# Streaming weights from DRAM copies whose sixteenths lie 144 KB apart instead of 32 KB

## The chip, the cores and the metric

The kernel runs on one core of one Trainium2 chip. The metric is the device time of one execution in microseconds (us). A core has a matrix engine (PE; its weight loads are listed as PEld), a vector engine (DVE), a scalar engine (ACT), GpSimd (POOL) and a sync engine (SP). DMAs are issued by SP, ACT and POOL and carried out by the core's 16 DMA engines.

## The reference, cut to what matters

Two networks read the same normalised input `xn` and their results are added to `x`. Network A is an attention with a recurrent memory: 64 segments of 32 rows are worked off one after the other, since the first 8 output rows of a segment are the memory of the next. Network B computes a small gated MLP for two of the 2048 rows, picked by a router.

```python
for s in range(n_seg):                                   # 64 segments
    h = concatenate([mem, xn[:, 32*s:32*(s+1), :]])      # 40 rows x 1024
    q, k, v = h @ Wq, h @ Wk, h @ Wv                     # each 1024 x (32 heads * 128)
    p = softmax(where(mask, q @ k.T * scale, -1e9))
    o = einsum((p @ v), Wo)                              # (32*128) x 1024
    mem = o[:, :8, :]
    outs.append(o[:, 8:, :])
return x + concatenate(outs) + B(xn)
```

All four weight matrices are needed in each segment, because segment s+1 cannot begin before segment s has given its memory rows. [...]

## The kernel before

The weights are cut into 64 granules of 128 partitions x 2048 bf16 (512 KB). Granules 0 to 47 are pieces of Wq, Wk and Wv (a 128-row piece of the contraction times half of the 4096 columns, in the order of `PHASES`), granules 48 to 63 are two heads of Wo each. 44 granules stay in SBUF from the first segment on (tiles `wres`). The other 20, named in `STREAMED`, come from DRAM again in each segment. One of these (6) is kept in PSUM as a whole and half of another (25) as well, so from segment 1 on 18 whole granules and one half granule (256 KB) are streamed: 19 DMAs a segment, 63 segments.

The streamed granules go through five SBUF slots (pool `wstream`, `N_SLOT`, tile `g`). `fetch` (line 346) takes the next entry of the list `flow` and issues one DMA on SP's queue. In segment 0 it reads from the weight matrix itself (line 353), later from a DRAM copy of the granule, `wsc` (line 355). The call comes from `after` (line 460), as soon as the program has written down the last matmul that reads the granule which holds the slot, so SP's next issue waits for that matmul: the order of the fetches is the order of use, at most five granules ahead.

The copies `wsc` are DRAM tiles, made once in segment 0 by `copy_block` (line 385), one DMA from DRAM to DRAM each on POOL's queue. Each is [128, 2048]: the row that goes to partition p is 4 KB long and lies 4 KB behind that of partition p-1, so a copy is one contiguous block of 512 KB, and the eight rows of one sixteenth of the partitions (32 KB) stand next to each other. In the weight matrices Wq, Wk and Wv the rows of a granule are 8 KB apart, so there the rows of one sixteenth begin 64 KB behind those of the one ahead.

In a segment PE goes through the granules in order: for each of the six phases eight granules with four matmuls of 128x512 each (line 802), then 16 granules of Wo with eight of 128x256 (line 575). In between stand the transposes, scores and sums of the attention, and the projections of the memory rows of the group of segments to come (lines 568 and 587). Besides the granules, each segment moves small things: the input rows (line 273, POOL), the output rows (line 872, POOL), and a spill of projected rows (`ql_d`: stored from line 617 on ACT's queue, read back by line 484 on POOL). After the last segment the MLP's weights are loaded (lines 406 and 409) and used.

Of the kernel before, what the change touches and what calls it, by code (L numbers as in the profile page):

```python
# [8 lines left out]
BF16 = mybir.dt.bfloat16  # L9
# [41 lines left out]
def kernel(  # L51
# [16 lines left out]
    nc = tc.nc  # L68
    P = 128
    Bsz, S, D = A_x.shape  # L70
# [19 lines left out]
    Wo2 = A_Wo.rearrange("h e d -> (h e) d")  # L90
# [11 lines left out]
    def granule_dram(g):  # L102
        if g < 48:
            p, kc = divmod(g, KC)
            mat, half = PHASES[p]
            return Wqkv[mat][kc * P:(kc + 1) * P, 2048 * half:2048 * (half + 1)]
        w = g - 48
        return Wo2[2 * w * P:(2 * w + 2) * P, :].rearrange("(hh e) d -> e hh d", hh=2)

    def granule_out(t, g):  # L110
        return t[:, :] if g < 48 else t.rearrange("p (hh d) -> p hh d", hh=2)
# [3 lines left out]
    dram = ctx.enter_context(tc.tile_pool(name="dram", bufs=1, space=DRAM))  # L115
# [13 lines left out]
    def columns(g, s):  # L129
        if s > 0 and g == KEPT_WHOLE:  # L130
            return None
        return slice(0, 1024 if s > 0 and g == KEPT_PART else 2048)

    wsc = {g: dram.tile([P, columns(g, 1).stop - columns(g, 1).start], BF16, name=f"wsc{g}")
           for g in streamed if g != KEPT_WHOLE}
    r_d = dram.tile([1, S], BF16, name="r_d")

# [59 lines left out]
    for s in range(4):  # L197
        nc.vector.tensor_copy(out=SELM[:, s, :, 0:XM],
                              in_=IDENT[:, 32 * s:32 * s + XM].unsqueeze(1).to_broadcast([P, 4, XM]))
        nc.vector.tensor_copy(out=SELL[:, s, :, :],  # L200
                              in_=IDENT.rearrange("p (s c) -> p s c", c=32)[:, :, XM:SEG])
# [144 lines left out]
    def fetch():  # L346
        if not flow:
            return
        s, g = flow.pop(0)
        t = wstream.tile([P, 2048], BF16, tag="g", name="g")  # L350
        c = columns(g, s)
        if s == 0:
            nc.sync.dma_start(out=granule_out(t, g), in_=granule_dram(g))
        elif c is not None:
            nc.sync.dma_start(out=t[:, c], in_=wsc[g][:, :])
        queued.append((g, t))

    def part(t, jq):
# [26 lines left out]
    def copy_block(g):  # L385
        c = columns(g, 1)
        if c is not None:
            src = granule_dram(g)
            nc.gpsimd.dma_start(out=granule_out(wsc[g], g), in_=src if g >= 48 else src[:, c])

    to_copy = list(streamed)
    flow += [(s, g) for s in range(NSEG) for g in streamed if s == 0 or g != KEPT_WHOLE]
# [38 lines left out]
    for g in range(48):  # L431
        if g in streamed:
            n_q += 1
            if n_q < N_SLOT:
                fetch()
            continue
        if n_q >= N_SLOT:
            break
        load_resident(g)
        if g % 2 == 1 and n_x < NT // 2:  # L440
            load_x(n_x)
            n_x += 1
# [17 lines left out]
    def after(s, g):  # L460

        if s == 0:
            if g in side:
                side[g]()
            if g % 2 == 1 and g >= 8 and to_copy:
                copy_block(to_copy.pop(0))
            if n_x_left and g % 2 == 1:
                load_x(n_x_left.pop(0))
            while todo_res and todo_res[0] <= g + 2 * 64 // n_str + 8 and (todo_res[0] < resident[-10] or g >= 2 * NT + 12):
                load_resident(todo_res.pop(0))  # L470
        if g in streamed and (s == 0 or g != KEPT_WHOLE):
            fetch()
        if s == NSEG - 1:
            if g in resident:
                free_homes.append(g)
            if not flow:
                fetch_moe()
# [143 lines left out]
    for s in range(NSEG):  # L621
# [172 lines left out]
        for p, (mat, half) in enumerate(PHASES):  # L794
# [3 lines left out]
            for kc in range(KC):  # L798
                g = 8 * p + kc
# [198 lines left out]
```

## Time and profile before

| | |
|---|---|
| time, median of 3 runs | 1875.73 us (1872.84 to 1882.51) |
| the profiled execution | 1878.39 us, span 1876.7 us |
| PE busy | 1572.0 us, 84% of the span |
| DVE, ACT, POOL busy | 885.9, 692.0, 452.5 us |
| moved by DMA | 712.29 MB, mean 380 GB/s |
| of it on SP's queue (q1) | 671.18 MB |
| fetches from `wsc` | 1134 of 512 KB and 63 of 256 KB |

The span is the time from the first to the last instruction; the profiled execution is 1.7 us longer than its span. The row of DMA gives the busy share of the 16 DMA engines in tenths in 40 slices of 46.9 us, the row of GB/s what they moved. A DMA is listed with the time that its issue takes on the engine that issues it, and with the time from issue to landing.

### The profile page before, as it was taken

The numbers are of one execution on the slowest core, as the hardware profiler recorded it, in microseconds if no ns is written. First come the engines' busy times: TensorE is split into PE (matmuls) and PEld (weight loads), VectorE is DVE, ScalarE is ACT, GpSimd is POOL, SyncE is SP. The second block draws the span as 40 slices with busy tenths as digits, with TensorE's granted clock in tenths as the row PEclk, the third lists the DMA queues.
The fourth block names the chain that finished last, engine by engine and source line by source line (L and its number), as shares of the span: only waits on it lengthen the run. The fifth ranks groups of instructions, "written<-read, shape, count | busy, mean of one in ns | idle before, by whom it ended". The sixth has DMA issues, their size and how long they took to land.

```text
span 1876.7 us, 80489 instructions
## 1 busy us (share of the span) xinstructions
PE 1572.0 (84%) x34976; PEld 850.8 (45%) x34976; DVE 885.9 (47%) x2929; ACT 692.0 (37%) x1948; POOL 452.5 (24%) x898
## 2 busy tenths in 40 slices
PE   3458898889888988899889988988888888888864
PEld 1124444444454444445454444444444444444433
DVE  6725544544455444544454454544554454445430
ACT  1113433443344343444343344434343344334320
POOL 3111322213131322213131322323132221312120
PEclk8669999999999999999999999999999999999995
DMA  9999999999999999999999999999999999999998
GB/s 370 405 353 385 373 379 381 384 372 375 397 382 398 367 389 390 385 383 380 382 376 390 366 397 379 387 392 373 371 383 382 372 382 380 370 381 368 368 404 329
DMA packets 232115, 712.29 MB, mean 380 GB/s; under 512 B 39296, under 2 KB 53168, under 8 KB 231760
## 3 DMA queue, kind: packets, MB, share of 16 engines
q1 hardware_dynamic: 194384, 671.18, 93.4%
q0 software_dynamic: 28736, 28.09, 4.7%
q10 hardware_dynamic: 8640, 7.87, 1.2%
q8 instruction: 274, 4.49, 0.9%
q14 instruction: 81, 0.66, 0.1%
HBM read 694.32 MB, written 22.29 MB: 382 GB/s over the span
## 4 chain that ended last, share of the span: by engine, by line
DMA 57%; PE 37%; DVE 3%; issue 1%; ACT 1%; SPq 1%; ACTq 0%; DVEq 0%
DMA g<-wsc 50%; PE PSm L802 20%; PE PSl L568 5%; PE WO L575 4%; PE BT L638 3%; DMA XP<-in_A_x_dram 2%; PE WL L587 2%; DMA MW<-in_B_w_gate_dram 1%; DVE XR L248 1%; DMA MW<-in_B_w_up_dram 1%; DMA g<-in_A_Wq_dram 1%; DMA wres<-in_A_Wo_dram 1%; DMA g<-in_A_Wo_dram 1%; DMA MW<-in_B_w_down_dram 1%; DMA g<-in_B_w_down_dram 1%
## 5 line engine op out<-in xcount | busy, mean ns | idle before, releaser
L802 PE MATMUL PSm<-wres,ST 128*32 128x512 bf16 x8448 | 704.9, 384 | 7.8 <-DMA wres<-in_A_Wv_dram 3.6
L802 PEld LDWEIGHTS <-ST 128*32 128x32 bf16 x12288 | 323.0, 96 | 417.9 <-issue 174.7
L802 PE MATMUL PSm<-g,ST 128*32 128x512 bf16 x3588 | 361.4, 387 | 100.9 <-DMA g<-wsc 77.8
L575 PEld LDWEIGHTS <-OT 128*32 128x32 bf16 x8192 | 220.5, 97 | 162.8 <-issue 137.7
L821 ACT CAST XB<-PSm 128x512 bf16<-128x512 f32 x256 | 150.6, 588 | 293.2 <-PE PSm L802 290.9
L575 PE MATMUL WO<-wres,OT 128*32 128x256 bf16 x5632 | 238.6, 278 | 16.0 <-DMA wres<-in_A_Wo_dram 8.0
L484 POOL DMA_DIRECT2D LX<-ql_d x63 | 33.6, 533 | 816.0 <-PE WO L575 366.1
L575 PE MATMUL WO<-g,OT 128*32 128x256 bf16 x2560 | 132.7, 281 | 80.1 <-DMA g<-wsc 70.2
L568 PE MATMUL PSl<-wres,STL 128*32 128x512 bf16 x2112 | 184.0, 389 | 0.3 <-issue 0.2
L872 POOL DMA_DIRECT2D out_dram<-X x256 | 129.5, 513 | 215.0 <-DVE X L870 169.7
L653 DVE COPY KT<-BT 128x512 bf16<-128x512 bf16 x112 | 45.9, 410 | 286.5 <-issue 186.8
L273 POOL DMA_DIRECT2D X<-in_A_x_dram x256 | 129.5, 510 | 190.3 <-PE PSm L802 68.6
L378 ACT COPY BK<-KEPT 128x512 bf16<-128x512 bf16 x126 | 74.4, 590 | 130.0 <-PE WO L575 102.0
L646 ACT COPY QT<-BT 128x512 bf16<-128x512 bf16 x128 | 75.0, 586 | 125.9 <-PE BT L491 74.1
L638 PEld LDWEIGHTS <-XB 128*128 128x128 bf16 x1024 | 58.4, 98 | 117.8 <-ACT XB L821 67.9
L638 PE MATMUL BT<-IDENT,XB 128*128 128x128 bf16 x1024 | 102.0, 222 | 9.2 <-ACT XB L821 7.8
L568 PEld LDWEIGHTS <-STL 128*32 128x32 bf16 x3072 | 84.5, 98 | 55.7 <-issue 10.6
L870 DVE TENSOR_TENSOR X<-WO,X 128x256 bf16<-128x256 f32 x64 | 27.2, 425 | 170.4 <-PE WO L575 170.4
L831 ACT CAST VM<-PSm 128x512 bf16<-128x512 f32 x128 | 76.0, 594 | 85.0 <-PE PSm L802 83.8
L724 PEld LDWEIGHTS <-VM 32*128 32x128 bf16 x2048 | 65.5, 91 | 85.3 <-issue 72.2
L382 DVE COPY g<-KEPT 128x512 bf16<-128x512 bf16 x126 | 47.7, 420 | 108.5 <-PE PSm L802 62.0
L670 DVE TENSOR_TENSOR BS<-BS,CT 128x96 f32<-128x96 f32 (+1 forms) x256 | 59.1, 231 | 77.1 <-PE BS L663 72.7
(173 smaller groups left out, 2363.5 us busy)
## 6 DMA issues: line engine op xcount, KB each, us to landing
g<-wsc SPq DMA_DIRECT2D x1134, 512.0 KB, 6.1
g<-wsc SPq DMA_DIRECT2D x63, 256.0 KB, 5.5
LX<-ql_d POOLq DMA_DIRECT2D x63, 128.0 KB, 5.9
ql_d<-XBl ACTq DMA_DIRECT2D x60, 128.0 KB, 5.7
MW<-in_B_w_gate_dram SPq DMA_DIRECT2D x16, 448.0 KB, 9.5
MW<-in_B_w_up_dram SPq DMA_DIRECT2D x16, 448.0 KB, 9.0
wres<-in_A_Wk_dram SPq DMA_DIRECT2D x12, 512.0 KB, 11.6
MW<-in_B_w_down_dram SPq DMA_DIRECT2D x12, 512.0 KB, 10.6
```

What stands on the lines that cost most here:

```text
L273: nc.gpsimd.dma_start(out=X[s % 2][32 * g:32 * g + XM, :], in_=x2[s * SEG:s * SEG + XM, 256 * g:256 * (g + 1)])
L378: copy(out=back[c][:, :], in_=KEPT_COLS[KEPT_WHOLE][c])
L568: nc.tensor.matmul(PSl[32 * jq:32 * jq + 32, :], lhsT=STL[:, g % KC, :], rhs=part(Gv, jq), start=first_, stop=last_, tile_position=(0, 32 ...
L575: nc.tensor.matmul(PS[32 * g:32 * g + 32, 0:256], lhsT=lhs(h), rhs=Gv[:, D * hs + 256 * g:D * hs + 256 * (g + 1)], start=(first and hs == ...
L638: nc.tensor.transpose(out=PTq[:, il, :, :].rearrange("p j r -> p (j r)"), in_=XB[:, il * P:(il + 1) * P], identity=IDENT[:, :])
L646: nc.scalar.copy(out=QT[half][:, :, :], in_=pv)
L670: nc.vector.tensor_tensor(out=S4, in0=S4, in1=m, op=ALU.add)
L724: nc.tensor.matmul(o, lhsT=VM[half][q0:q0 + 32, il * P:(il + 1) * P], rhs=PTm[q0:q0 + 32, il, 0:NK], start=True, stop=False, tile_position ...
L802: nc.tensor.matmul(PSm[32 * jq:32 * jq + 32, :], lhsT=ST[:, kc, :], rhs=part(Gv, jq), start=(kc == 0), stop=(kc == KC - 1), tile_position= ...
L821: nc.scalar.copy(out=XB[:, :], in_=PSm[:, :])
L831: nc.scalar.copy(out=VM[half][:, :], in_=PSm[:, :])
L872: nc.gpsimd.dma_start(out=out2[s * SEG:s * SEG + XM, 256 * g:256 * (g + 1)], in_=OB[32 * g:32 * g + XM, :])
```

## The change

The DRAM copies get another shape. Each is now allocated as [16, 36, columns], of which rows 0 to 7 of each 36 are used. The eight rows of one sixteenth of the partitions stay contiguous (8 x 4 KB), and the next sixteenth begins 36 x 4 KB = 144 KB behind (72 KB for the half granule, whose rows are 2 KB; there it was 16 KB). The fetch reads the same 128 rows in the same order. The source of its DMA is now a pattern of three levels (16 x 8 x row) instead of two (128 x row). The copies of Wq, Wk and Wv granules stay one DMA each; those of the five Wo granules become two DMAs each, one for each of the two heads.

```diff
-    wsc = {g: dram.tile([P, columns(g, 1).stop - columns(g, 1).start], BF16, name=f"wsc{g}")
+
+    wsc = {g: dram.tile([16, 36, columns(g, 1).stop - columns(g, 1).start], BF16, name=f"wsc{g}")[:, 0:8, :]
            for g in streamed if g != KEPT_WHOLE}
...
         elif c is not None:
-            nc.sync.dma_start(out=t[:, c], in_=wsc[g][:, :])
+            nc.sync.dma_start(out=t[:, c], in_=wsc[g])
...
         if c is not None:
-            src = granule_dram(g)
-            nc.gpsimd.dma_start(out=granule_out(wsc[g], g), in_=src if g >= 48 else src[:, c])
+            if g >= 48:
+                w = g - 48
+                src = Wo2[2 * w * P:(2 * w + 2) * P, :].rearrange("(hh a b) d -> a b hh d", hh=2, b=8)
+                for hh in range(2):
+                    nc.gpsimd.dma_start(out=wsc[g][:, :, D * hh:D * (hh + 1)], in_=src[:, :, hh, :])
+            else:
+                nc.gpsimd.dma_start(out=wsc[g], in_=granule_dram(g)[:, c].rearrange("(a b) c -> a b c", b=8))
```

No instruction changes its place among the others of its engine. What changes is the form of the DMAs. On POOL, at the end of segment 0, the last copies stand so before the change (a row is the line, the destination, the source and the destination's pattern; `wsc_119` to `wsc_123` are the five Wo granules, `RROW` is the router's row):

```order
L389 DMA wsc_117<-in_A_Wv_dram 128x2048
L389 DMA wsc_118<-in_A_Wv_dram 128x2048
L389 DMA wsc_119<-in_A_Wo_dram 256x1x1024
L389 DMA wsc_120<-in_A_Wo_dram 256x1x1024
L260 DMA RROW<-r_d 1x16x128
L389 DMA wsc_121<-in_A_Wo_dram 256x1x1024
```

and so with it:

```order
L395 DMA wsc_117<-in_A_Wv_dram 16x8x2048
L395 DMA wsc_118<-in_A_Wv_dram 16x8x2048
L393 DMA wsc_119<-in_A_Wo_dram 16x8x1024 x2
L393 DMA wsc_120<-in_A_Wo_dram 16x8x1024 x2
L261 DMA RROW<-r_d 1x16x128
L393 DMA wsc_121<-in_A_Wo_dram 16x8x1024 x2
```

The five Wo copies are ten DMAs now, each with runs of 2 KB, 128 of them instead of 256. On SP, the first fetches of segment 1 stand so before the change (`wsc_105` to `wsc_109` are the first five streamed granules):

```order
L353 DMA g<-in_A_Wo_dram 128x2x1024
L355 DMA g<-wsc_105 128x2048
L355 DMA g<-wsc_106 128x2048
L355 DMA g<-wsc_107 128x2048
L355 DMA g<-wsc_108 128x2048
L355 DMA g<-wsc_109 128x2048
```

and so with it:

```order
L353 DMA g<-in_A_Wo_dram 128x2x1024
L356 DMA g<-wsc_105 128x1x2048
L356 DMA g<-wsc_106 128x1x2048
L356 DMA g<-wsc_107 128x1x2048
L356 DMA g<-wsc_108 128x1x2048
L356 DMA g<-wsc_109 128x1x2048
```

The order is the same; each of the 1197 fetches carries a level more in its patterns.

## The prediction

> **What bounds the kernel now.** I read the page first: the span, the busy engines, the rows of DMA and GB/s, the biggest queue, the chain that ended last, and the DMA issues.
>
> ```profile
> span 1876.7 us, 80489 instructions
> ...
> PE 1572.0 (84%) x34976; PEld 850.8 (45%) x34976; DVE 885.9 (47%) x2929; ACT 692.0 (37%) x1948; POOL 452.5 (24%) x898
> ...
> DMA  9999999999999999999999999999999999999998
> GB/s 370 405 353 385 373 379 381 384 372 375 397 382 398 367 389 390 385 383 380 382 376 390 366 397 379 387 392 373 371 383 382 372 382 380 370 381 368 368 404 329
> ...
> q1 hardware_dynamic: 194384, 671.18, 93.4%
> q0 software_dynamic: 28736, 28.09, 4.7%
> q10 hardware_dynamic: 8640, 7.87, 1.2%
> ...
> DMA 57%; PE 37%; DVE 3%; issue 1%; ACT 1%; SPq 1%; ACTq 0%; DVEq 0%
> ...
> g<-wsc SPq DMA_DIRECT2D x1134, 512.0 KB, 6.1
> g<-wsc SPq DMA_DIRECT2D x63, 256.0 KB, 5.5
> ```
>
> No engine is full (PE 84%), but the 16 DMA engines are at nine tenths or more in all slices but the last, and SP's queue alone takes 93.4% of them. The chain goes through DMA for 57% of the span, nearly all of it fetches from `wsc`. The slices are not alike, though: with the DMA engines busy throughout, the second slice, in segment 0, moves 405 GB/s, and those of the streamed part 366 to 398. So what counts is not whether a DMA engine has work, but how long it takes for a packet.
>
> The view of waits says how much of this PE feels.
>
> ```profile
> PE PSm L802 <- DMA g<-wsc: 77.8, 170, 2.3
> ...
> PE WO L575 <- DMA g<-wsc: 70.2, 145, 1.7
> ```
>
> PE waits 148.0 us in all for `wsc` data. That is what a perfect memory could win as long as PE's own work stays as it is. SP's queue shows the same loop from the other side:
>
> ```profile
> SPq L355 <- PE PSm L802: 448.1, 656, 4.1
> SPq L355 <- DMA g<-wsc: 385.3, 740, 2.6
> ```
>
> SP mostly waits for a slot of the five to come free: for a matmul that still reads it (448.1 us for the largest group), or, on the row with DMA as the releaser, with the last fetch of that slot. The third view is of the fetch line itself, with the duration of its issue (min/median/max, ns) and then the time to landing of all DMAs that it issues (us):
>
> ```profile
> L355 SPq DMA_DIRECT2D g<-wsc x1197: 319/320/1167, 119.9 to 1808.5; - x200
> ...
> DMA to landing us min/median/max: 3.3/6.0/10.6
> ```
>
> From the first issue at 119.9 us to the last at 1808.5 us are 1688.6 us for 1197 fetches, 1.41 us each. A slot comes round every 5 x 1.41 = 7.05 us; 6.0 of these are between issue and landing, though the quickest fetch lands after 3.3 us. So 2.7 us of a typical fetch is waiting in line in the DMA engines: **the kernel is bound by the DMA engines' rate in the 63 streamed segments**, with PE close behind.
>
> **What the rate depends on.** The windows view gives, for each stretch, the PE busy time in its second and third column and, at the end, DMA share and GB/s. The first two stretches lie in segment 0 (loads from Wq, Wk and Wv), the third and fourth in the streamed part, the last in the loads of the MLP's gate and up weights.
>
> ```profile
> 35.00:60.00 25.00, 11.82 (x161) 4.77 (x154) 17.55 (x43) 2.87 (x8) 5.80 (x12) 0.65 1.03 412
> 60.00:85.00 25.00, 10.78 (x118) 4.39 (x115) 22.99 (x46) 4.46 (x8) 6.33 (x11) 0.76 1.03 400
> 500.00:900.00 400.00, 358.85 (x8144) 195.26 (x8140) 194.28 (x662) 161.92 (x459) 103.20 (x202) 1.00 1.01 385
> 1000.00:1400.00 400.00, 358.07 (x8033) 192.54 (x8023) 191.08 (x646) 159.82 (x454) 100.67 (x198) 0.99 1.01 382
> 1826.00:1842.00 16.00, 6.63 (x228) 6.37 (x229) 3.25 (x14) 2.97 (x4) 1.13 (x2) 0.50 1.03 403
> ```
>
> At a DMA share of 1.01 to 1.03 in all five, the streamed part moves 382 to 385 GB/s, the others 400 to 412. In the streamed part PE is busy 358.07 us of 400 (89.5%). Finer, the 25 us of segment 0 between 35 and 60 us, in 40 slices:
>
> ```profile
> DMA  9999999999999999999999999999999999999999
> GB/s 406 423 413 390 393 429 410 413 410 426 416 416 423 410 419 426 413 420 419 419 420 420 419 426 374 400 382 423 418 416 419 420 419 433 393 387 380 393 419 419
> ```
>
> and 27 us of the streamed part, about one segment:
>
> ```profile
> DMA  9999989898988999999999999999999999999999
> GB/s 425 425 413 394 413 346 388 328 249 328 340 322 273 255 328 370 382 388 425 346 352 388 425 408 408 407 366 426 394 432 413 411 420 405 382 382 364 352 352 364
> ```
>
> In the first most slices stand near 419, though the POOL queue writes copies of 512 KB meanwhile, and the lowest is 374. In the second some slices reach 425 too, but for eight slices, 5.4 us, it drops to 249 to 340. So the engines can do 419 or more in both, and what the streamed part loses is lost in drops. There are two differences. Segment 0 reads rows 8 KB apart, whose sixteenths are 64 KB apart; the MLP's rows are 7 KB apart (3584 columns of bf16), its sixteenths 56 KB; only the copies are read as one block with sixteenths 32 KB apart. And the streamed part has the small loads and stores of each segment beside it, and only five fetches in line, so that one late engine holds back a slot.
>
> **The change part by part.**
>
> Spacing of the sixteenths. It removes no byte and no packet: the rows are still 4 KB, 128 to a fetch. Its whole worth is in the rate. If the spacing causes all drops, the streamed part runs at the mean of the other three stretches, (412 + 400 + 403) / 3 = 405 GB/s: 1688.6 x (1 - 382/405) = 96 us less. That is under the 148.0 us that PE waits, so PE would let it through. With nothing of it due to the spacing it is 0. I take the middle, 393.5 GB/s, because one of the two differences goes away and the other stays: 1688.6 x (1 - 382/393.5) = **49 us less**. PE then still waits some 99 us for data, so the DMA rate stays the bound and no new wait has to appear. No row of this trace shows a spacing of 144 KB; the nearest are 56 and 64 KB on one side and 32 KB on the other. Below nothing is possible as well: a fetch now touches a range of 16 x 144 KB = 2.25 MB instead of 0.5 MB, and the worst steady slices of the page, 366 to 368 GB/s, are the price that I put on that (1688.6 x (382/367 - 1) = 69 us more).
>
> [...]
>
> Issue on SP. The 1197 fetches have a source of three levels now. The trace has no three-level DMA on SP of just this form; the nearest are the loads of Wo in segment 0 (three levels on both sides) and the last two stores, whose DRAM side depends on a register:
>
> ```profile
> L145 SPq DMA_DIRECT2D wres<-in_A_Wo_dram x11: 368/469/4302, 88.8 to 117.2; - x11
> ...
> DMA to landing us min/median/max: 6.5/12.9/20.0
> ```
>
> ```profile
> L962 SPq DMA_DIRECT2D out_dram<-T x2: 579/642/704, 1871.8 to 1873.9; - x2
> ```
>
> The issue, 320 ns now, lies between 320 and 704 ns by these rows. SP has 1.41 us for each fetch, so it isn't the bound even at 704. The 384 ns more come into the slot's round of 7.05 us, where the 2.7 us in line at the DMA engines cover them: I take 0. If the cover fails (an empty line, as in the drops), the price is at most 384 ns for every fifth fetch, 1197 x 0.384 / 5 = 92 us; half of that where the issue takes 0.5 us. Behind a waiting fetch on SP there are only further fetches, so nothing else is delayed.
>
> Copies on POOL. They run once, in segment 0:
>
> ```profile
> L389 POOL DMA_DIRECT2D wsc<-in_A_Wv_dram x6: 515/530/750, 62.3 to 92.3; - x6
> L389 POOL DMA_DIRECT2D wsc<-in_A_Wo_dram x5: 699/823/953, 92.8 to 98.0; - x5
> ```
>
> ```profile
> L484 POOL DMA_DIRECT2D LX<-ql_d x63: 528/528/549, 120.1 to 1787.4; - x63
> ```
>
> Three-level patterns on POOL take 528 ns (the read-back of `ql_d`), like the two-level copies (530), so 14 copies stay as they are. The five Wo copies at 823 ns become ten at some 530: 5 x (2 x 530 - 823) = 1.2 us more on POOL around 95 us, when POOL has little to do (it is busy 24% of the span). The same bytes are written. The first Wo copy is the fifteenth fetch of segment 1, at 119.9 + 14 x 1.41 = 140 us, some 40 us after its copy was issued. I take 0; without that cover it is 1.2 us.
>
> Sum: -49 + 0 + 0. The profiled execution took 1878.4 us (the span and 1.7 us around it), so it would take 1829; the median of the runs shown is 2.7 us lower than that execution, so the forecast is **1826 us**.
>
> **The rivals.**
>
> Not the spacing. The drops may come from the other difference: the small stores and loads of each segment, and five slots that make one late engine hold back all. For it: in segment 0, where the rate is high, far more stands in line (12.9 us to landing by the row of line 145, against 6.0), so a late engine keeps nobody waiting. Against: the small transfers, on the queues q0 and q10, take 4.7 and 1.2% of the DMA engines, and the drops last for 5 us in a row. Nor need the change do what it says: the trace doesn't show which engine carries which row, and an engine may not be given eight neighbouring rows. In both cases the time stays, 1876 us. [...]
>
> Slower through scattered rows. The block of 512 KB is read by 16 engines that are close together in memory; after the change each of them works 144 KB from the next. If the memory serves neighbours better, the rate falls to what the worst steady slices show, 367 GB/s, and the time is 1876 + 69 = 1945 us. It decides as soon as the mean rate in the streamed part falls under 382. Against it: segment 0 reads over 1 MB a granule (128 rows, 8 KB apart) and is faster, not slower.
>
> Slower through the issue. If a three-level fetch takes 0.5 to 0.7 us to issue and the line at the DMA engines is empty as often as the drops suggest, half to all of the 92 us comes on top: 1876 + 46 = 1922 us. It is the bound outright only from 1.41 us a fetch. Against it: the 2.7 us in line.
>
> All of it. If the drops go altogether, the time is 1876 - 96 = 1780 us.
>
> **How the numbers follow.** The forecast, some of the drops gone, has 0.45, the case that all go 0.14, no change 0.15, scattered rows 0.14, the issue 0.12. Within 0.5% (about what a measurement of this kernel can tell from no change) is 1866 to 1885. The forecast's case lies between 1790 and 1866, so faster gets 0.59, same 0.15, slower 0.26. To leave out no more than 0.2, the range goes from 1775, which leaves out about a third of the case that all go, to 1915, which takes in the issue at half its cover and the lighter half of the scattered rows. The likeliest one's own range is 1790 to 1866.
>
> **What would show it.** In the streamed part the windows view should read about 393 GB/s at the same DMA share, the eight low slices of a segment should be fewer and shallower, PE's waits for `wsc` should fall from 148.0 to about 99 us, and the chain's share of DMA with it. The median time to landing should stay near 6 us if slots still are the limit, or fall. The issue on line 356 shows its own duration; anything up to 0.7 us with a rate over 382 clears it. The prediction is wrong if the rate stays at 382 (not the spacing), falls under 382 with an issue of 320 ns (scattered rows), or if the issue grows and DMA share falls under 1.0 (the issue).

## The result, and the profile after

The change makes the kernel slower by a third: 2541.95 us (median of 6 runs, 2513.01 to 2574.03) against 1882.62 us before in the same series; the ratio is 1.346, 95% interval 1.340 to 1.352. It leaves out the slowest of the six executions (2574.03 us), which was in the chip's slower state. The forecast was 1826 us.

The page of the changed kernel (the execution of 2513.01 us), in the rows that stood in the prediction for the kernel before:

```profile
span 2511.4 us, 80500 instructions
...
PE 1761.9 (70%) x34976; PEld 932.1 (37%) x34976; DVE 901.7 (36%) x2929; ACT 698.3 (28%) x1948; POOL 456.0 (18%) x903
...
DMA  9999999999999999999999999999999999999999
GB/s 379 400 248 311 280 277 275 310 269 288 260 265 279 272 303 271 275 274 268 271 262 270 269 264 272 295 280 280 275 263 264 266 278 271 271 278 295 321 251 346
...
q1 hardware_dynamic: 194384, 671.18, 96.3%
...
DMA 85%; PE 12%; DVE 1%; issue 1%; SPq 0%; ACT 0%; DVEq 0%
...
g<-wsc SPq DMA_DIRECT2D x1134, 512.0 KB, 9.1
```

The same bytes go over the same queue, and the row of DMA is as full as before. What fell is the row of GB/s, and only where the copies are read: the first two slices (segment 0) show 379 and 400, the last, with the MLP's weights, 346; the 37 in between, which were 353 to 404, are at 248 to 321. The chain is now DMA for 85%.

The waits of PE for the copies, 148.0 us before:

```profile
PE PSm L808 <- DMA g<-wsc: 441.8, 600, 2.0
...
PE WO L581 <- DMA g<-wsc: 167.0, 225, 2.5
```

They are 608.8 us, 460.8 more. PE's own busy time grew by 189.9 us (1761.9 against 1572.0, at a mean granted clock of 0.887 against 0.957). Together that is 650.7 us, and the spans differ by 634.7, so PE's other idle time shrank by 16.0 us.

The fetch line, with its issue (ns) and the time to landing (us):

```profile
L356 SPq DMA_DIRECT2D g<-wsc x1197: 514/514/1548, 119.2 to 2440.0; - x200
...
DMA to landing us min/median/max: 6.0/9.1/14.6
```

From first to last issue are 2320.8 us, 1.94 us a fetch in place of 1.41. That is 632 us more, so nearly the whole loss lies in the streamed part. The issue takes 514 ns and not 320, but lies far below 1.94 us. In the windows view (DMA share and GB/s at the end) stand a stretch of segment 0 and two of the streamed part:

```profile
20.00:100.00 80.00, 40.88 (x533) 18.00 (x526) 60.79 (x133) 11.56 (x27) 18.85 (x35) 0.70 1.03 407
600.00:1000.00 400.00, 290.52 (x5844) 152.94 (x5840) 143.00 (x477) 118.19 (x333) 75.93 (x149) 0.91 1.03 277
1000.00:1400.00 400.00, 287.60 (x5642) 151.18 (x5635) 135.90 (x445) 113.59 (x314) 67.91 (x135) 0.90 1.03 271
```

Loads from the weight matrices, which the change doesn't touch, still run at 407 GB/s. The fetches from the copies keep the DMA engines as busy (1.03) and move 271 to 277 GB/s where it was 382 to 385: **each row of 4 KB takes longer in the DMA engine that carries it**. The trace has this directly, since it keeps the time of every packet: of the packets of 4 KB that start between 600 and 1400 us, the median took 245 ns, and 159 ns in the kernel before. In segment 0 it is 159 ns in both.

### The profile page after: what moved, and what is told of

Its sections match the earlier page's. It is cut to its first block, busy times and chain, and to the rows that moved or that the text cites. A ratio compares the mean times of both kernels' runs of the same rounds, so it can differ in the third digit from the quotient of the medians.

```text
span 2511.4 us, 80500 instructions
## 1 busy us (share of the span) xinstructions
PE 1761.9 (70%) x34976; PEld 932.1 (37%) x34976; DVE 901.7 (36%) x2929; ACT 698.3 (28%) x1948; POOL 456.0 (18%) x903
## 3 DMA queue, kind: packets, MB, share of 16 engines
q1 hardware_dynamic: 194384, 671.18, 96.3%
## 4 chain that ended last, share of the span: by engine, by line
DMA 85%; PE 12%; DVE 1%; issue 1%; SPq 0%; ACT 0%; DVEq 0%
DMA g<-wsc 80%; PE PSm L808 6%; PE WO L581 3%; PE PSl L574 2%; DMA XP<-in_A_x_dram 1%; DMA MW<-in_B_w_gate_dram 1%; DVE XR L249 1%; DMA MW<-in_B_w_up_dram 1%; DMA g<-in_A_Wq_dram 1%; PE WL L593 1%; DMA g<-in_A_Wo_dram 1%; DMA wres<-in_A_Wo_dram 1%; DMA g<-in_B_w_down_dram 0%; PE BT L294 0%; DMA MW<-in_B_w_down_dram 0%
## 5 line engine op out<-in xcount | busy, mean ns | idle before, releaser
L808 PE MATMUL PSm<-wres,ST 128*32 128x512 bf16 x8448 | 725.1, 393 | 5.8 <-DMA wres<-in_A_Wv_dram 2.6
L808 PE MATMUL PSm<-g,ST 128*32 128x512 bf16 x3588 | 375.3, 403 | 463.1 <-DMA g<-wsc 441.8
L808 PEld LDWEIGHTS <-ST 128*32 128x32 bf16 x12288 | 346.1, 97 | 847.6 <-issue 632.4
L581 PEld LDWEIGHTS <-OT 128*32 128x32 bf16 x8192 | 264.7, 113 | 293.7 <-issue 248.9
L581 PE MATMUL WO<-wres,OT 128*32 128x256 bf16 x5632 | 301.9, 336 | 13.8 <-DMA wres<-in_A_Wo_dram 8.3
L581 PE MATMUL WO<-g,OT 128*32 128x256 bf16 x2560 | 159.5, 332 | 179.4 <-DMA g<-wsc 167.0
L574 PE MATMUL PSl<-wres,STL 128*32 128x512 bf16 x2112 | 197.4, 416 | 0.1
L739 DVE CAST OT<-BT 128x128 bf16<-128x128 f32 x128 | 37.3, 292 | 281.1 <-PE BT L732 167.5
L739 ACT CAST OT<-BS 128x128 bf16<-128x128 f32 x128 | 34.1, 266 | 262.4 <-PE BT L732 139.8
```

What stands on the lines that cost most here:

```text
L574: nc.tensor.matmul(PSl[32 * jq:32 * jq + 32, :], lhsT=STL[:, g % KC, :], rhs=part(Gv, jq), start=first_, stop=last_, tile_position=(0, 32 ...
L581: nc.tensor.matmul(PS[32 * g:32 * g + 32, 0:256], lhsT=lhs(h), rhs=Gv[:, D * hs + 256 * g:D * hs + 256 * (g + 1)], start=(first and hs == ...
L739: copy(out=OT[half][:, 2 * ph + jl, :, :], in_=ov[:, :, 0:SEG])
L808: nc.tensor.matmul(PSm[32 * jq:32 * jq + 32, :], lhsT=ST[:, kc, :], rhs=part(Gv, jq), start=(kc == 0), stop=(kc == KC - 1), tile_position= ...
```

## The experiments

Two theories can do this. The *address theory* is the prediction's rival of scattered rows: the place of the rows in memory slows the reads. The *dealing theory* says that the place doesn't matter. The fetch's source has become a pattern of three levels with 16 entries in the outermost, where it was 128, and the DMA engines are dealt their rows by that level (each gets its share of the entries); in the new dealing they get in each other's way. The first four kernels set spacing and pattern apart. For each run the rows are the windows view of two stretches of the streamed part. Where a ratio is given, the kernel was executed several times beside the kernel before; the others were executed once.

**Spacing alone.** Rows 18 KB apart, so the sixteenths are 144 KB apart, with a pattern of two levels:

```diff
-    wsc = {g: dram.tile([P, columns(g, 1).stop - columns(g, 1).start], BF16, name=f"wsc{g}")
+    wsc = {g: dram.tile([P, 9 * columns(g, 1).stop // 2], BF16, name=f"wsc{g}")[:, 0:columns(g, 1).stop]
```

> Every row of a copy begins 18 KB behind the one ahead, so the sixteenths are 144 KB apart as in the change, but the fetch keeps the pattern of two levels (128 x row). Address theory (the place in memory slows the reads): the streamed part moves 270 to 300 GB/s, the time is 2300 to 2550 us, the issue on SP stays 320 ns. Dealing theory (a pattern whose outermost level has 16 entries gives each DMA engine other rows and partitions than one of 128 entries, and the engines get in each other's way, wherever the rows lie): 375 to 405 GB/s as before the change, 1800 to 1890 us. What is left of my own forecast: if the spacing of the sixteenths is worth anything by itself, this run is under 1866 us.

```profile
600.00:1000.00 400.00, 351.00 (x7977) 190.83 (x7969) 190.03 (x646) 160.00 (x454) 102.63 (x201) 1.00 1.01 380
1000.00:1400.00 400.00, 350.71 (x7944) 189.68 (x7943) 188.93 (x638) 156.83 (x446) 93.81 (x186) 0.99 1.00 375
```

Measured: 1887.06 us, ratio to before 1.0026 (0.9998 to 1.0054), 375 to 380 GB/s. So the 144 KB are innocent, and worth nothing either: the address theory falls, and with it the gain that I had forecast.

**Pattern almost alone.** The change with 9 rows in place of 36, sixteenths 36 KB apart:

```diff
-    wsc = {g: dram.tile([16, 36, columns(g, 1).stop - columns(g, 1).start], BF16, name=f"wsc{g}")[:, 0:8, :]
+    wsc = {g: dram.tile([16, 9, columns(g, 1).stop - columns(g, 1).start], BF16, name=f"wsc{g}")[:, 0:8, :]
```

> The change with 9 rows in place of 36: the sixteenths are 36 KB apart, 4 KB more than before the change, and the pattern is 16 x 8 x row. Dealing theory: as slow as the change, 265 to 290 GB/s and 2450 to 2600 us, issue 514 ns. Address theory: nearly the block of before, so 360 to 385 GB/s and 1870 to 1960 us.

```profile
600.00:1000.00 400.00, 292.42 (x5868) 154.29 (x5868) 142.40 (x470) 116.33 (x327) 70.32 (x140) 0.91 1.03 277
1000.00:1400.00 400.00, 289.26 (x5653) 151.39 (x5643) 140.94 (x466) 115.82 (x324) 69.21 (x136) 0.89 1.03 271
```

Measured: 2559.14 us, the same rates as the change, issue 514 ns. The dealing theory holds: the loss is there with a spacing of only 4 KB more than before.

**Another outermost level.** Blocks of four rows, 20 KB apart:

```diff
-    wsc = {g: dram.tile([16, 36, columns(g, 1).stop - columns(g, 1).start], BF16, name=f"wsc{g}")[:, 0:8, :]
+    wsc = {g: dram.tile([32, 5, columns(g, 1).stop - columns(g, 1).start], BF16, name=f"wsc{g}")[:, 0:4, :]
```

(and `b=4` for `b=8` in the copies)

> The copies lie in blocks of four rows, 20 KB apart, and the pattern is 32 x 4 x row: three levels, but the outermost has 32 entries. Dealing theory in its plain form (each DMA engine gets a run of neighbouring entries of the outermost level, here two blocks, the same eight neighbouring partitions as in the change): as slow as the change, 265 to 290 GB/s, 2450 to 2600 us. If 32 entries are dealt as finely as 128 are: 375 to 405 GB/s, 1830 to 1900 us. Address theory: rows still close together, so 360 to 385 GB/s, 1870 to 1960 us.

```profile
600.00:1000.00 400.00, 346.03 (x7684) 187.16 (x7672) 180.19 (x607) 152.75 (x428) 98.57 (x195) 0.98 0.99 366
1000.00:1400.00 400.00, 343.74 (x7736) 184.74 (x7732) 189.27 (x638) 155.15 (x442) 94.57 (x186) 1.00 1.00 369
```

```profile
L356 SPq DMA_DIRECT2D g<-wsc x1197: 512/513/1178, 119.3 to 1862.6; - x200
```

Measured: 1932.35 us, 366 to 369 GB/s. Three levels are not the trouble by themselves: with 32 entries outermost nearly all of the loss is gone. My plain form of the theory, by which two neighbouring blocks go to one engine, is wrong: it gave 2450 to 2600 us. 32 entries behave as 128 do, or nearly (I had given 375 to 405 GB/s for that, so the rate is a miss too). The time lies in the range that I gave for the address theory, but by chance: with the sixteenths 144 KB apart, below, the time is the same.

**The prediction's reading of segment 0.** Rows 8 KB apart, as in the weight matrices:

```diff
-    wsc = {g: dram.tile([P, columns(g, 1).stop - columns(g, 1).start], BF16, name=f"wsc{g}")
+    wsc = {g: dram.tile([P, 2 * columns(g, 1).stop], BF16, name=f"wsc{g}")[:, 0:columns(g, 1).stop]
```

> Every row of a copy begins 8 KB behind the one ahead, as in the weight matrices that segment 0 reads at 400 to 412 GB/s; two levels. My forecast's reading (the block of neighbouring rows causes the drops of the streamed part): 390 to 410 GB/s, 1770 to 1850 us. Its rival (the drops come from the five slots and the small transfers): 380 to 385 GB/s, 1860 to 1890 us.

```profile
600.00:1000.00 400.00, 340.91 (x7697) 185.08 (x7696) 183.83 (x622) 153.75 (x439) 91.40 (x181) 1.00 0.99 364
1000.00:1400.00 400.00, 341.53 (x7650) 186.47 (x7653) 182.13 (x614) 151.78 (x428) 100.36 (x197) 0.99 0.99 365
```

Measured: 1962.53 us, ratio 1.042 (1.040 to 1.045), 364 to 365 GB/s. A miss for both: the layout on which I had based the gain is not faster in the streamed part but slower. The high rate of segment 0 doesn't come from its pitch.

What in the dealing costs the time? The next four kernels ask how many engines carry a fetch, and which partitions it writes.

**Eight entries outermost.** The change with blocks of 16 rows:

```diff
-    wsc = {g: dram.tile([16, 36, columns(g, 1).stop - columns(g, 1).start], BF16, name=f"wsc{g}")[:, 0:8, :]
+    wsc = {g: dram.tile([8, 18, columns(g, 1).stop - columns(g, 1).start], BF16, name=f"wsc{g}")[:, 0:16, :]
```

(and `b=16` for `b=8` in the copies)

> The change with blocks of 16 rows: the pattern is 8 x 16 x row, blocks 72 KB apart, so the sixteenths are 32 KB or 40 KB apart. Dealing theory (the outermost level of the pattern is what is dealt to the DMA engines): only eight DMA engines get rows of a fetch, DMA share falls to 0.5 to 0.6, at most 200 GB/s, over 3200 us. If rows are dealt to the engines whatever the pattern's levels are: DMA share stays at 1.0 and the time is 1880 to 2600 us.

```profile
600.00:1000.00 400.00, 259.08 (x4434) 131.93 (x4427) 105.95 (x353) 88.34 (x249) 54.53 (x107) 0.77 0.53 210
1000.00:1400.00 400.00, 260.69 (x4374) 130.07 (x4367) 106.18 (x351) 87.32 (x245) 57.61 (x114) 0.76 0.53 209
```

Measured: 3266.23 us, DMA share 0.53, 209 to 210 GB/s (a little over the 200 that I gave). That is what eight engines at work give: SP's queue takes 51.7% of the time of the 16 engines, and it has 184808 packets in place of the 194384 of the change, 8 fewer for each of the 1197 fetches. So the outermost level seems to be what is dealt. And the eight that work, if it is eight, are not slow: 210 / 8 = 26 GB/s each, against 382 / 16 = 24 before and 277 / 16 = 17 in the change; a packet of 4 KB takes 159 ns in the median, as before the change. If each carries one entry, it did no harm here that an engine has a run of 16 neighbouring rows and writes 16 neighbouring partitions.

**Which partitions.** Copies as before the change, but each fetch as two DMAs, of partitions 0 to 63 and 64 to 127:

```diff
-            nc.sync.dma_start(out=t[:, c], in_=wsc[g][:, :])
+            for h in range(2):
+                nc.sync.dma_start(out=t[64 * h:64 * h + 64, c], in_=wsc[g][64 * h:64 * h + 64, :])
```

> Copies as before the change (one block, two levels), but each fetch is two DMAs, of partitions 0 to 63 and 64 to 127, rows of 4 KB as ever. [...]

```profile
600.00:1000.00 400.00, 278.47 (x5001) 126.37 (x5000) 124.05 (x416) 101.30 (x287) 66.81 (x129) 0.81 0.99 236
1000.00:1400.00 400.00, 274.78 (x4960) 126.14 (x4960) 118.53 (x392) 98.50 (x278) 59.51 (x117) 0.82 0.98 233
```

The same two DMAs for the even and the odd partitions (`t[h:P:2, c]` from `wsc[g][h:P:2, :]`):

> As the run with the halves, but the two DMAs of a fetch take the even and the odd partitions. [...]

```profile
600.00:1000.00 400.00, 319.21 (x6598) 155.83 (x6590) 158.94 (x531) 132.32 (x371) 82.67 (x163) 0.91 0.88 312
1000.00:1400.00 400.00, 317.30 (x6699) 156.46 (x6700) 160.74 (x542) 132.78 (x379) 81.03 (x159) 0.92 0.90 317
```

```profile
L356 SPq DMA_DIRECT2D g<-wsc x2394: 450/541/1773, 118.7 to 2154.0; - x200
```

And for the left and the right half of the columns (`t[:, n * h:n * h + n]` from the same columns of `wsc[g]`, n half of them):

> As the run with the halves, but the two DMAs of a fetch take the left and the right half of the columns, 128 rows of 2 KB each. It has their number of DMAs without their partitions. All theories: a little slower than before through 2 KB pieces and two issues, 345 to 385 GB/s, 1880 to 2080 us. If it is as slow as the halves, then not the partitions but the second DMA of a fetch makes them slow.

```profile
600.00:1000.00 400.00, 348.06 (x7353) 180.43 (x7353) 178.03 (x596) 145.78 (x415) 88.45 (x175) 1.00 1.00 351
1000.00:1400.00 400.00, 355.60 (x7464) 184.32 (x7460) 179.37 (x607) 150.25 (x425) 96.18 (x187) 0.98 1.00 353
```

Measured: 2936.85 us for the halves, 2222.66 us for even and odd, 2010.46 us for the columns. The second DMA of a fetch costs little (351 to 353 GB/s with the columns). The halves have two levels and a plain block in memory, and still full engines (0.98 to 0.99) move 233 to 236 GB/s: it is the set of 64 partitions that goes with the loss, which points to the way into SBUF and not to memory. One other difference is left: a half is also a range of 256 KB in DRAM and not of 512. But the change reads over 2.25 MB and is slow too, so a narrow range can't be the reason for both. Even and odd are another case: the DMA share is 0.88 to 0.90, and 317 / 0.90 = 352 GB/s at full share is just the rate of the columns (353 / 1.00). The packets aren't slow: 159 ns in the median. The engines wait, in part for the two issues of 541 ns, and more for something else that the view of SP's waits shows:

```profile
SPq L356 <- DMA ql_d<-XBl: 238.8, 60, 5.6
```

SP stood still 60 times, 238.8 us in all, until a store of `ql_d` from ACT's queue had landed; in the kernel before these waits are 1.1 us. The halves have them too (315.9 us); why was not tried. So with two levels, the rows of 64 partitions spread over SBUF are not slowed (159 ns).

**The dealing on the spread partitions.** Even and odd once more, but from blocks of nine rows, so that the outermost level has 16 entries (`out=t[h:P:2, c], in_=wsc[g][:, h:8:2, :]` on copies of `[16, 9, columns]`):

> As the run with even and odd partitions in two DMAs, but the source is a pattern of 16 x 4 x row (blocks of nine rows, 36 KB), so that the outermost level has 16 entries. [...] If the sixteen entries did no harm by themselves: like the two-level run, 312 to 317 GB/s at 0.88 to 0.90, 2190 to 2260 us.

```profile
600.00:1000.00 400.00, 295.00 (x5920) 141.49 (x5921) 144.17 (x485) 119.58 (x338) 76.24 (x149) 0.90 0.95 282
1000.00:1400.00 400.00, 296.45 (x5784) 140.36 (x5780) 136.83 (x451) 115.02 (x320) 68.44 (x136) 0.87 0.94 275
```

Measured: 2491.48 us, 275 to 282 GB/s at a share of 0.94 to 0.95. The partitions, the number of DMAs and the bytes are those of the two-level run with even and odd; the outermost level is another, and the loss is back: 2491 in place of 2223 us, and 282 / 0.95 = 297 GB/s at full share in place of 352. The issues (515 ns against 541) are no longer than those of the two-level run and the engines have fewer gaps (0.95 against 0.88 to 0.90), so gaps between the fetches don't make the difference; a row takes 213 ns in the median against 159. The copies lie in blocks 36 KB apart here; but no change of the place in DRAM alone made the rows slow in any run (159 ns in the median with rows 18 or 8 KB apart).

**The change's spacing, dealt finer.** Blocks of four rows 72 KB apart, so that two blocks, one sixteenth, begin 144 KB behind the two ahead:

```diff
-    wsc = {g: dram.tile([16, 36, columns(g, 1).stop - columns(g, 1).start], BF16, name=f"wsc{g}")[:, 0:8, :]
+    wsc = {g: dram.tile([32, 18, columns(g, 1).stop - columns(g, 1).start], BF16, name=f"wsc{g}")[:, 0:4, :]
```

(and `b=4` for `b=8` in the copies)

> The spacing of the change, dealt finer: blocks of four rows 72 KB apart, so that the sixteenths (two blocks) are 144 KB apart, pattern 32 x 4 x row, three levels. Dealing theory: as the run with blocks of four rows 20 KB apart, whatever the spacing: 365 to 372 GB/s, 1915 to 1945 us, issue 513 ns; the 50 us over the time before are then the longer issue (1197 x 0.193 / 5 = 46 us). Address theory: the change's spacing slows the reads, under 340 GB/s, over 2050 us.

```profile
600.00:1000.00 400.00, 351.58 (x7898) 189.98 (x7898) 189.73 (x642) 158.89 (x447) 100.64 (x196) 0.99 1.00 374
1000.00:1400.00 400.00, 347.32 (x7712) 188.62 (x7712) 181.77 (x612) 154.09 (x434) 94.54 (x187) 0.98 1.00 369
```

Measured: 1927.49 us, ratio to before 1.024 (1.019 to 1.029), 369 to 374 GB/s, issue 513 ns, like the 20 KB blocks. So the spacing is out, with three levels too. What remains over the time before, some 43 us, fits the 46 us of the longer issue; no run lengthened the issue alone, so that part is argued, not shown.

Put together: in every run with 16 entries outermost the rows are slow, and of the others only in the halves. The median time of a packet of 4 KB between 600 and 1400 us says it for all runs at once: 159 ns before the change, with rows 18 and 8 KB apart, with both kinds of blocks of four, with eight entries and with even and odd; 245 in the change and with sixteenths 36 KB apart, 213 with even and odd from 16 entries, 274 with the halves. (The columns have packets of 2 KB.)

Why 16 entries do it was not shown. If the entries are dealt one to an engine, each DMA engine of the change carries one block of eight rows into eight neighbouring partitions. That the engines then get in each other's way on the way into SBUF was my assumption. The halves speak for it: from a plain block in memory into 64 neighbouring partitions a row takes 274 ns, into 64 spread ones 159. In the change it takes 245, and nearly all rows are slowed (only 5% took 170 ns or less). The run with eight entries doesn't fit: there too, dealt so, a block of neighbouring rows goes into neighbouring partitions, and at 26 GB/s an engine and 159 ns a row no collision is to be seen; why was not tried. No run shows directly which engine carried which row, since the trace doesn't name engines.

## Why the prediction was wrong

**What bounds the kernel: right.** The rate of the DMA engines in the streamed part sets the time; it fell to 271 to 277 GB/s, and 632 of the 634.7 us appeared there, at a DMA share of 1.03 against 1.01.

**The spacing, -49 us: wrong, and the step that failed.** "It removes no byte and no packet: the rows are still 4 KB, 128 to a fetch. Its whole worth is in the rate." I looked for the rate in the addresses alone. The new layout also changed the form of the pattern, and I counted that only as time on SP; for what it does to a packet, the sum has no term. The spacing is worth nothing, with two levels (1.0026) or with three (20 KB and 72 KB blocks alike), which is the 0 that I had set as one end; the outermost level of 16 is worth more than 600 us, since a row of 4 KB takes 245 ns in place of 159. The inference behind the 49 us was wrong too: from segment 0's 400 to 412 GB/s I concluded that its pitch of 8 KB is better, and at that pitch the streamed part ran at 364 to 365, and the kernel was 4.2% slower. Two stretches that differ in several things had been read as if they differed in one. What makes the drops in the streamed part of the kernel before stays open; it is not the block of neighbouring rows.

**The issue, 0: right for the change.** It is 514 ns, between my bounds of 320 and 704, and the DMA engines have no gap from it (share 1.03). But that is partly luck: the line in front of slowed engines is longer (9.1 us to landing, not 6.0), so the change is no test of the cover that I counted on. Where the engines aren't slowed otherwise, the cover seems to fail: the 43 us of the finer dealing are about the full price by my formula (1197 x 0.193 / 5 = 46).

**The copies on POOL, 0: right.** The rows of the copy line show ten Wo copies of some 530 ns, as taken:

```profile
L393 POOL DMA_DIRECT2D wsc<-in_A_Wo_dram x10: 532/532/538, 93.0 to 104.3; - x10
L395 POOL DMA_DIRECT2D wsc<-in_A_Wv_dram x6: 524/540/548, 62.5 to 92.5; - x6
```

**The rivals.** Scattered rows had the right sign and the wrong mechanism, and its 69 us more are about a tenth of the measured loss. The rival that the change need not do what it says stood at the right place ("the trace doesn't show which engine carries which row"), but I priced it at nothing ("In both cases the time stays, 1876 us"): I took it that another dealing would merely make the spacing meaningless. That nothing had no row behind it: all loads of that trace on SP have 128 entries outermost, so no row of it bounded a pattern with 16, and the range should have stayed open upwards.

## What to carry to other kernels

When a layout in DRAM changes, compare the form of the DMA's pattern on both sides before its addresses: the outermost level went here with the share of the DMA engines that a fetch keeps busy (0.53 with 8 entries, 0.99 to 1.03 with 16, 32 and 128) and with the time of a row in them (245 ns with 16, 159 ns with 8, 32 and 128), where a fetch is one DMA. Engines whose packets are slowed still looked busy: the sign of it was a DMA share of 1.03 at 271 to 277 GB/s, where it had been 382 to 385, and then the time of a packet is the number to look at. Padding that keeps 128 rows outermost cost nothing at a row pitch of 18 KB (ratio 1.0026) and 4.2% at 8 KB, and blocks of four rows cost some 2.5%; blocks of eight cost a third.

## What the runs showed of the hardware that I had not expected

- Fetches whose outermost level has 8 entries kept the DMA engines busy for a share of 0.53 (209 to 210 GB/s), as eight of the 16 would.
- Loads of 64 neighbouring partitions at a time moved 233 to 236 GB/s with full engines (274 ns for a row of 4 KB); loads of 64 spread ones 312 to 317 with engines that had gaps (159 ns).
- With two DMAs a fetch, SP waited 315.9 us (halves) and 238.8 us (even and odd) in all for stores on ACT's queue to land, against 1.1 us in the kernel before.
- An issue on SP takes 320 ns for 128 rows in two levels, some 513 ns for 16 x 8 and 32 x 4, 577 ns for 8 x 16, by the row of the fetch line in that run:

```profile
L356 SPq DMA_DIRECT2D g<-wsc x1197: 577/577/757, 117.1 to 3188.1; - x200
```

- With a row pitch of 8 KB in the copies the kernel is 4.2% slower than with rows that follow each other (364 to 365 GB/s in the streamed part against 382 to 385); with one of 18 KB it is not.
